# Batch 0's second group of heads goes in front of all other tasks, u's squares by halves, more casts on GpSimd, other ranks

## The chip, the cores and the metric

One core of one Trainium2 chip runs the kernel as one program. The time is the device time of an execution in microseconds, the median of several; lower is better. Engines are named as in the profile: PE (TensorE, matmuls), PEld (its weight loads), DVE (VectorE), ACT (ScalarE), POOL (GpSimd) and SP (SyncE, which issues the DMAs).

## The reference

Three stages in sequence. Attention with a forget gate over 4 batches, 8 heads, 576 positions and 64 columns; then a token and channel mixer; then a gated convolution block:

```python
scores = scale * np.matmul(q, k.transpose(0, 1, 3, 2))
decay = cum[:, :, :, None] - cum[:, :, None, :]        # cum: running sum of log f
scores = np.where(causal, -1000000000.0, scores + decay)
attn = np.exp(scores - max); attn = attn / (sum + 1e-09)
x = (attn @ v), heads side by side: (4, 576, 512)

h = np.maximum(xt @ w_tok1, 0.0) @ w_tok2              # xt: x with positions last; 576 -> 256 -> 576
u = x + h.transpose(0, 2, 1)
x = u + np.maximum(u @ w_ch1, 0.0) @ w_ch2             # 512 -> 1536 -> 512

h = np.maximum(x @ w_in, 0.0)                          # 512 -> 1024
gate = 1.0 / (1.0 + np.exp(-conv_out))                 # conv_out: 3 taps along the positions
out = (h * gate) @ w_out                               # 1024 -> 512
```

(The lines are shortened to what is computed.)

## The kernel before

All large products are made of float16 parts: every factor is split into a high part (a cast) and a low part (what the cast left), and `mm3` (L280 to L284) issues three matmuls for one: high by high (L282), high by low (L283), low by high (L284).

**Heads.** The 32 heads come in pairs (`pair`), and four heads make a group; two groups make a batch. A head's scores come from PE (L1004, L1008); DVE takes a masked maximum by row block (L1022, output t and m); ACT takes the exponential (L1028). Heads 0 to 7 (batch 0) are transposed by PE in float32. For later heads POOL casts t to its high part ph in two pieces of 1024 and 640 columns (`hi_part`, L1037), DVE makes the low part pl in the same two pieces (`lo_part`, L1043), and SP transposes both by DMA. PE multiplies by the group's values (PV; L1093 for heads 0 to 7, L1098 to L1100 later). DVE divides by the row sums (`norm`, L1107, L1108) and writes the head's part of x (`xout`, L1116, tile xf). x is then split: xh by POOL (L274) for heads below `XHP` = 8 and by ACT (L271) for the others, xl by POOL (L277), and POOL scales xf in place (`x_scale`, L1138). The group's values vp are split by POOL as well: three casts (L274) and three subtractions (L916).

**Groups.** `group(g)` holds the token mixer. Its first product T1 needs the xh and xl of four heads; T2 the two halves of T1's output. `u_copy` (ACT, L1261) takes T2 out of PSUM into us, `u_squares` (ACT, L1270, output junk) sums the squares of 1152 columns into one column of um. After a batch's second group `u_span` lets PE spread um's two columns over the partitions (the helper at L262, one matmul for each column), and `u_scale` (DVE, L251 to L257) makes a power of two of them, by which ACT (L610, uh) and DVE (L613, ul) split u.

**Channel mixer.** It runs in three parts of the 1536 columns. For one part M1 multiplies u by five column blocks of w_ch1; its output r is taken out of PSUM by ACT (high, L662) and DVE (low, L666). M2 multiplies r by the five row blocks of w_ch2. The weights of a part are staged by `weight_set`: loaded by SP, decoded by ACT (L319) and DVE (L323, L324), squared for their scale (L520), then scaled and split. For batch 0's first part the ch1 weights are scaled, cast and split by POOL (L555, L274, L277; five blocks, into the slots w10, w0, w1, w2, w3), the ch2 weights by ACT (L570) and DVE (L574; slots w4 to w8).

**What sets the order.** Each step is a task with an engine, an estimated time, a rank, and what it reads and writes. The class `Order` at the top plays the tasks through: in `run` each engine offers the open task that can start first, ties going to the lower rank, and the earliest offer of all engines is taken. The tasks are then emitted in that order, so every engine has one fixed queue, and an instruction whose input is late holds up all that stand behind it. Ranks of a head grow with its number; a group's tasks have t0 = (4g + 3) * `PER` + 6. `SETR` and `LATER` are added to t0 for the staging of the weights: `SETR` for batch 0's first part (ch1, ch2), `LATER` for the batches' further parts, and the steps 4.0 and 2.5 in the call of `weight_set` spread the five blocks.

## Time and profile before

| what | us |
|---|---|
| three runs | 717.93, 715.51, 716.53 |
| median | 716.53 |
| the profiled execution | 717.09 |
| its span, first to last instruction | 715.3 |
| PE busy | 693.4 |
| DVE busy | 501.8 |
| ACT busy | 429.7 |
| POOL busy | 266.2 |

The profiled execution is one further run; its trace gives starts and durations of all instructions in microseconds from the span's start. In a row `out<-in` are the names of the tiles, then partitions x elements and types. Where an engine sat idle before an instruction, the square brackets say how long and what released it. A busy PE counts from the start of a matmul to its modelled end; matmuls that follow each other start 0.12 us apart at 288 columns though each is shown with 0.29.

### The profile page before, as it was taken

The numbers are of one execution on the slowest core, as the hardware profiler recorded it, in microseconds if no ns is written. First come the engines' busy times: TensorE is split into PE (matmuls) and PEld (weight loads), VectorE is DVE, ScalarE is ACT, GpSimd is POOL, SyncE is SP. The second block draws the span as 40 slices with busy tenths as digits, with TensorE's granted clock in tenths as the row PEclk, the third lists the DMA queues.
The fourth block names the chain that finished last, engine by engine and source line by source line (L and its number), as shares of the span: only waits on it lengthen the run. The fifth ranks groups of instructions, "written<-read, shape, count | busy, mean of one in ns | idle before, by whom it ended". The sixth has DMA issues, their size and how long they took to land.

```text
span 715.3 us, 16400 instructions
## 1 busy us (share of the span) xinstructions
PE 693.4 (97%) x6417; PEld 559.4 (78%) x6417; DVE 501.8 (70%) x1255; ACT 429.7 (60%) x942; POOL 266.2 (37%) x344
## 2 busy tenths in 40 slices
PE   7999897799999999999999999999999999999998
PEld 6888676587778787887888778778878778778786
DVE  5778989998876788436666856635778866875570
ACT  5777886576845685555674544312177766676671
POOL 2145898657682867230000222102023222323240
PEclk9999999999999999999999999999999999999999
DMA  9435899799995987875454855345211121100101
GB/s 203 148 93 176 212 275 186 143 249 244 231 225 123 220 165 178 220 256 157 151 180 124 284 187 164 100 134 160 66 42 58 51 59 35 57 20 26 34 18 51
DMA packets 152974, 101.99 MB, mean 143 GB/s; under 512 B 89984, under 2 KB 145024, under 8 KB 152896
## 3 DMA queue, kind: packets, MB, share of 16 engines
q1 hardware_dynamic: 152896, 100.94, 54.6%
q8 instruction: 50, 0.82, 0.5%
q14 instruction: 28, 0.23, 0.1%
HBM read 57.73 MB, written 23.59 MB: 114 GB/s over the span
## 4 chain that ended last, share of the span: by engine, by line
PE 82%; DVE 7%; POOL 5%; ACT 2%; issue 2%; DMA 1%; SPq 0%; DVEq 0%; POOLq 0%; ACTq 0%
PE w L282 14%; PE w L283 14%; PE w L284 14%; PE z L283 8%; PE z L282 8%; PE z L284 8%; PE z L1004 5%; PE w L1093 3%; PE w L1245 2%; POOL vp L916 2%; PE z L1008 1%; POOL vp L274 1%; DVE pl L1043 1%; ACT t L1028 1%; PE w L1099 1%
## 5 line engine op out<-in xcount | busy, mean ns | idle before, releaser
L284 PEld LDWEIGHTS <-w 128*128 128x128 f16 x1280 | 125.3, 98 | 34.9 <-DVE w L574 3.2
L282 PEld LDWEIGHTS <-w 128*128 128x128 f16 x1280 | 124.9, 98 | 34.4 <-issue 2.7
L283 PEld LDWEIGHTS <-w 128*128 128x128 f16 x1280 | 125.0, 98 | 34.3 <-issue 3.5
L282 PE MATMUL w<-uh,w 128*128 128x288 f16 x416 | 119.0, 286 | 1.2 <-DVE r L666 1.2
L284 PE MATMUL w<-uh,w 128*128 128x288 f16 x416 | 119.0, 286 | 0.0
L283 PE MATMUL w<-ul,w 128*128 128x288 f16 x416 | 119.0, 286 | 0.0
L277 POOL TENSOR_TENSOR g<-sg,g 128x286 f16<-128x286 f32 (+1 forms) x64 | 55.1, 867 | 150.2 <-ACT g L271 148.5
L1530 DVE SCALAR_TENSOR_TENSOR cv<-hp,cw,cv 128x286 f32<-128x286 f32 (+1 forms) x128 | 75.1, 594 | 38.2 <-ACT cv L1524 36.0
L662 ACT ACTIVATE r<-w 128x288 f16<-128x288 f32 x96 | 39.2, 408 | 87.9 <-PE w L284 87.7
L1028 ACT ACTIVATE t<-t,m 128x576 f32<-128x576 f32 (+4 forms) x160 | 81.3, 552 | 17.3 <-DVE m L1022 17.2
L739 POOL TENSOR_TENSOR p<-p,u 128x288 f32<-128x288 f32 x32 | 27.3, 883 | 150.1 <-DVE wraw L323 78.1
L1022 DVE CUSTOM_DVE_ANT_0 t<-z,mask 128x576 f32<-128x576 f32 (+4 forms) x160 | 69.9, 478 | 11.1 <-PE z L1008 11.0
L666 DVE SCALAR_TENSOR_TENSOR r<-w,r 128x288 f16<-128x288 f32 x96 | 43.4, 453 | 47.4 <-ACT r L662 46.6
L283 PE MATMUL z<-g,w 128*128 128x286 f16 (+1 forms) x256 | 73.3, 286 | 0.0
L282 PE MATMUL z<-g,w 128*128 128x286 f16 (+1 forms) x256 | 73.0, 285 | 0.0
L284 PE MATMUL z<-g,w 128*128 128x286 f16 (+1 forms) x256 | 72.9, 285 | 0.0
L284 PE MATMUL w<-vh,w 128*128 128x288 f16 x224 | 64.1, 286 | 0.0
L282 PE MATMUL z<-r,w 128*128 128x288 f16 x224 | 64.1, 286 | 0.0
L283 PE MATMUL w<-vl,w 128*128 128x288 f16 x224 | 64.1, 286 | 0.0
L284 PE MATMUL z<-r,w 128*128 128x288 f16 x224 | 64.1, 286 | 0.0
L282 PE MATMUL w<-vh,w 128*128 128x288 f16 x224 | 64.1, 286 | 0.0
L283 PE MATMUL z<-r,w 128*128 128x288 f16 x224 | 64.1, 286 | 0.0
(206 smaller groups left out, 1699.8 us busy)
## 6 DMA issues: line engine op xcount, KB each, us to landing
wraw<-in_moe_w_ch_dram SPq DMA_DIRECT2D x24, 512.0 KB, 4.7
qk<-in_qk_dram SPq DMA_DIRECT2D x16, 608.0 KB, 5.1
u_d<-us SPq DMA_DIRECT2D x8, 576.0 KB, 4.5
p_d<-res SPq DMA_DIRECT2D x32, 144.0 KB, 3.6
p<-p_d SPq DMA_DIRECT2D x8, 576.0 KB, 5.4
u<-u_d SPq DMA_DIRECT2D x8, 576.0 KB, 4.9
x_d<-p SPq DMA_DIRECT2D x8, 576.0 KB, 3.4
u<-x_d SPq DMA_DIRECT2D x8, 576.0 KB, 3.9
```

What stands on the lines that cost most here:

```text
L277: nc.gpsimd.tensor_tensor(o, a, b, ALU.subtract)
L282: nc.tensor.matmul(ps, wh, xh, start=(first and i == 0), stop=False)
L283: nc.tensor.matmul(ps, wh, xl, start=False, stop=False)
L284: nc.tensor.matmul(ps, wl, xh, start=False, stop=(last and i == n - 1))
L662: nc.scalar.activation(out=t[:, 0, :], in_=box["z", m], func=AF.Relu)
L666: nc.vector.scalar_tensor_tensor(t[:, 1, :], box["z", m], 0.0, f32(t[:, 0, :]), ALU.max, ALU.subtract)
L739: nc.gpsimd.tensor_tensor(box["p"][:, d], box["p"][:, d], box["u"][:, d], ALU.add)
L1004: nc.tensor.matmul(out_[x], t[r, Q0[i]:Q0[i] + 128], t[r, k0:k0 + n], start=first, stop=False)
L1022: nc.vector.tensor_tensor_reduce(to, z_t.pop((n, i)), mk, -0.125, 3e38, ALU.add, ALU.min, m_t[n][0:rows, i:i + 1])
L1028: nc.scalar.activation(out=tt[0:rows, o:o + w], in_=tt[0:rows, o:o + w], func=AF.Exp, bias=m_t[n][0:rows, i:i + 1], scale=-1.0)
L1093: nc.tensor.matmul(o[:, 0:65], p32(n)[:, 128 * blk:128 * blk + 128], vp32_t[g % 2][:, slot, hh, :], start=(j == 0), stop=(j == nb - 1))
L1530: nc.vector.scalar_tensor_tensor(cv, hp_t[m][:, s0 + t:s1 + t], cw[:, t, m:m + 1], cv, ALU.mult, ALU.add)
```

## The change

It has five parts.

1. `Order` gets a table `WAIT` by engine, all of it 0.0, and `run` picks in two steps: the earliest possible start on the engine plus `WAIT`, and among the tasks that can start by then the one of lowest rank.
2. `AHEAD` = 60 is taken from the rank of batch 0's second group (g == GB - 1, heads 4 to 7): of the heads' PV, norm, xout, xh, xl and scaling, and of t0 in `group`.
3. `XHP` is 12 in place of 8: the xh of heads 8 to 11 is made by POOL.
4. `SETR` is (10, 30) in place of (-20, 0) with steps of 2.0 in place of 4.0 and 2.5; `LATER` is (0, 30, 50) in place of (-30, 10, 30).
5. `u_squares` runs for each half of u (576 columns) with a column of um of its own; `u_span` spreads four columns and `u_scale` sums 512.

```diff
+    WAIT = {"PE": 0.0, "DVE": 0.0, "ACT": 0.0, "POOL": 0.0, "SP": 0.0, "-": 0.0}
...
-                pick = None
+                starts = []
                 for k in ks:
                     r = ready[k]
                     if takes[k]:
                         r = max(r, slot(k))
-                    if r >= far:
-                        continue
-                    c = (max(r, at), self.tasks[k][2], k)
-                    if pick is None or c < pick:
-                        pick = c
-                if pick and (best is None or pick[0] < best[0]):
-                    best = (pick[0], pick[2], e)
+                    if r < far:
+                        starts.append((max(r, at), self.tasks[k][2], k))
+                if not starts:
+                    continue
+
+                until_ = min(starts)[0] + self.WAIT[e]
+                pick = min((c[1], c[0], c[2]) for c in starts if c[0] <= until_)
+                if best is None or pick[1] < best[0]:
+                    best = (pick[1], pick[2], e)
...
-    XHP = 8
+    AHEAD = 60.0
+    XHP = 12
-    SETR = ((-20.0, 0.0),)
-    LATER = (-30.0, 10.0, 30.0)
+    SETR = ((10.0, 30.0),)
+    LATER = (0.0, 30.0, 50.0)
...
-    um = [const.tile([128, GB], F32, name=f"um{b}") for b in range(B)]
+    um = [const.tile([128, GB * NDM], F32, name=f"um{b}") for b in range(B)]
...
+                if g == GB - 1:
+                    rank -= AHEAD
...
-            nc.scalar.activation(out=junk[:, 0:NDM * S], in_=tok[g]["u"].rearrange("p d s -> p (d s)"), func=AF.Square,
-                                 accum_out=um[g // GB][:, g % GB:g % GB + 1])
+            at = NDM * (g % GB) + d
+            nc.scalar.activation(out=junk[:, 0:S], in_=tok[g]["u"][:, d], func=AF.Square,
+                                 accum_out=um[g // GB][:, at:at + 1])
...
-            um_t[b] = spread(um[b], GB)
+            um_t[b] = spread(um[b], GB * NDM)
-            power_of_root(su[b], um_t[b], 128 * GB, 2.0)
+            power_of_root(su[b], um_t[b], 128 * GB * NDM, 2.0)
...
+            if g == GB - 1:
+                t0 -= AHEAD
...
+                T("ACT", 0.8, t0 + 4, u_squares, g, d, reads=[("us", g % 2, d, e) for e in range(2)],
+                  writes=[("junk",), ("um", b, half, d)], pools=A1)
-            T("ACT", 1.15, t0 + 4, u_squares, g, reads=uk, writes=[("junk",), ("um", b, half)], pools=A1)
...
-                                [q + 4.0 * k for k in range(n)], [q + 4.0 * n + 2.5 * k for k in range(n)], factor, ONP[y])
+                                [q + 2.0 * k for k in range(n)], [q + 2.0 * n + 2.0 * k for k in range(n)], factor, ONP[y])
```

What that does to the queues shows at three places. Lines of the kernel after are 5 higher from about L250 on, and 7 to 11 higher behind L1250; the numbers behind the tiles' names differ between the two.

**POOL, while batch 0's channel weights are split and the heads of batch 1 begin.** ph is the high part of a head (first head 10, from t2, then head 11, from t3), w0 to w3 are weights of ch1, vp the values of a group (vp1: group 3), xh, xl and xf heads 8 to 11. Before:

```order
L277 TENSOR_TENSOR w0_113<-w1_114,w0_113 128x512
L1037 TENSOR_SCALAR ph_1385<-t2_190 128x1024
L274 TENSOR_SCALAR w1_114<-w2_115 128x512
L1037 TENSOR_SCALAR ph_1385<-t2_190 128x640
L277 TENSOR_TENSOR w1_114<-w2_115,w1_114 128x512
L277 TENSOR_TENSOR xl_1490<-xf_1433,xh_1486 128x5x64
L274 TENSOR_SCALAR w2_115<-w3_116 128x512
L1138 TENSOR_SCALAR xf_1433<-xf_1433,tac_218 128x5x64
L277 TENSOR_TENSOR w2_115<-w3_116,w2_115 128x512
L1037 TENSOR_SCALAR ph_1540<-t3_191 128x1024
L274 TENSOR_SCALAR w3_116<-w4_117 128x512
L1037 TENSOR_SCALAR ph_1540<-t3_191 128x640
```

After, two pieces that follow each other:

```order
L1042 TENSOR_SCALAR ph_1447<-t2_190 128x1024
L282 TENSOR_TENSOR w0_113<-w1_114,w0_113 128x512
L279 TENSOR_SCALAR xh_1484<-xf_1471 128x5x64 x2
L282 TENSOR_TENSOR xl_1497<-xf_1471,xh_1484 128x5x64 x2
L1143 TENSOR_SCALAR xf_1471<-xf_1471,tac_218 128x5x64 x2
```

```order
L279 TENSOR_SCALAR w1_114<-w2_115 128x512
L1042 TENSOR_SCALAR ph_1447<-t2_190 128x640
L282 TENSOR_TENSOR w1_114<-w2_115,w1_114 128x512
L560 TENSOR_SCALAR w3_116<-w3_116,pw_c10_226 128x512
L279 TENSOR_SCALAR vp1_201<-vf_1331 64x4x64 x2
L279 TENSOR_SCALAR vp1_201<-vf_1331 128x16x64
L921 TENSOR_TENSOR vp1_201<-vf_1331,vp1_201 64x4x64 x2
L921 TENSOR_TENSOR vp1_201<-vf_1331,vp1_201 128x16x64
L279 TENSOR_SCALAR w2_115<-w3_116 128x512
L560 TENSOR_SCALAR w4_117<-w4_117,pw_c10_226 128x512
L282 TENSOR_TENSOR w2_115<-w3_116,w2_115 128x512
L1042 TENSOR_SCALAR ph_1656<-t3_191 128x1024
```

The xh of heads 8 and 9 stands in POOL's queue now, and the six instructions of group 3's values, which stood nine rows behind the low part written to w2, stand ahead of it and of head 11's ph.

**DVE, at the low part pl of head 11 (from t3).** r is the output of M1, xf a head's part of x, wraw and w8, w9 weights of ch2 being decoded, the lines with m the score maxima. Before:

```order
L1043 SCALAR_TENSOR_TENSOR pl_1527<-t2_190,ph_1385 128x1024
L666 SCALAR_TENSOR_TENSOR r_1522<-w_1492,r_1522 128x288
L1116 TENSOR_TENSOR xf_1433<-w_1397,rs_1513 128x5x64
L1043 SCALAR_TENSOR_TENSOR pl_1527<-t2_190,ph_1385 128x640
L1043 SCALAR_TENSOR_TENSOR pl_1557<-t3_191,ph_1540 128x1024
L666 SCALAR_TENSOR_TENSOR r_1548<-w_1516,r_1548 128x288
L666 SCALAR_TENSOR_TENSOR r_1572<-w_1544,r_1572 128x288
```

After:

```order
L1027 ISA m_1310 128x1
L328 TENSOR_SCALAR wraw_1562<-wraw_1562 128x512
L329 SCALAR_TENSOR_TENSOR w9_122<-w9_122,wraw_1562 128x512
L1027 ISA t2_190,m_1653<-z_1631,mask_131 128x576
L1027 ISA m_1653 128x1
L543 TENSOR_REDUCE stat_c20_227<-stat_c20_227 128x1
L1048 SCALAR_TENSOR_TENSOR pl_1675<-t3_191,ph_1656 128x1024
```

Head 11's pl followed head 10's at once; now decoding of weights and score maxima of batch 1's next heads stand ahead of it.

**PE, around group 2's first token matmul T1 (xh, xl by w1h, w1l).** w4 to w8 hold ch2's weights: r by them is M2; qk, dec and sel make scores. Before:

```order
L284 LDWEIGHTS w8_121
L284 MATMUL w_1891<-r_1635,w8_121 128x288
L1004 MATMUL z_1922<-qk1_149 128x64 x2
L1004 MATMUL z_1922<-qk1_149 128x448 x2
L1008 MATMUL z_1922<-dec_133,sel_134 128x512 x2
L1004 MATMUL z_1934<-qk1_149 128x192 x2
L1004 MATMUL z_1934<-qk1_149 128x320 x2
L1008 MATMUL z_1934<-dec_133,sel_134 128x512 x2
L282 LDWEIGHTS w1h_212
L282 MATMUL w_1948<-xh_1486,w1h_212 128x256
L283 LDWEIGHTS w1h_212
L283 MATMUL w_1948<-xl_1490,w1h_212 128x256
```

After:

```order
L287 LDWEIGHTS w1h_212
L287 MATMUL w_1966<-xh_1484,w1h_212 128x256
L288 LDWEIGHTS w1h_212
L288 MATMUL w_1966<-xl_1497,w1h_212 128x256
L289 LDWEIGHTS w1l_213
L289 MATMUL w_1966<-xh_1484,w1l_213 128x256
L287 LDWEIGHTS w4_117
L287 MATMUL w_1991<-r_1492,w4_117 128x288
L288 LDWEIGHTS w4_117
L288 MATMUL w_1991<-r_1492,w4_117 128x288
L289 LDWEIGHTS w4_117
L289 MATMUL w_1991<-r_1492,w4_117 128x288
```

Before, the M2 triples of the part (r by w4 to w8, the last of them here) end ahead of T1; now T1 ends ahead of the first M2 triple.

## Rows read from the trace of the kernel before

**Rows 1.** The page: span, then busy time, share and instructions of each engine.

```profile
span 715.3 us, 16400 instructions
...
PE 693.4 (97%) x6417; PEld 559.4 (78%) x6417; DVE 501.8 (70%) x1255; ACT 429.7 (60%) x942; POOL 266.2 (37%) x344
```

**Rows 2.** Table of stretches: length, busy PE PEld DVE ACT POOL (instructions), clock, DMA.

```profile
80.00:100.00 20.00, 16.83 (x136) 13.11 (x135) 17.21 (x48) 16.80 (x35) 19.17 (x25) 1.00 1.02 256
100.00:120.00 20.00, 15.49 (x188) 12.28 (x189) 19.48 (x44) 12.71 (x26) 17.08 (x17) 1.00 1.01 228
120.00:141.00 21.00, 17.19 (x206) 13.25 (x203) 20.07 (x47) 12.23 (x27) 15.08 (x14) 1.00 0.72 131
...
142.00:250.00 108.00, 106.28 (x1282) 85.37 (x1281) 85.69 (x258) 72.91 (x151) 69.81 (x71) 1.00 1.00 217
```

**Rows 3.** Timeline of PE: start, us, instruction, [idle before <-releaser].

```profile
86.99 0.27 PE L283 MATMUL w<-xl,w1h 128*128 128x256 f16 x1 [2.65 <-POOL xl L277]
...
100.16 0.49 PE L262 MATMUL w<-ident,um 128*128 128x128 f32 x2 [0.68 <-ACT junk L1270]
...
113.31 0.46 PE L262 MATMUL w<-ident,vacc 128*128 128x128 f32 x2 [2.48 <-DVE r L666]
...
117.15 0.28 PE L282 MATMUL w<-uh,w 128*128 128x288 f16 x1 [1.18 <-DVE r L666]
...
131.07 0.30 PE L284 MATMUL w<-r,w 128*128 128x288 f16 x1 [2.93 <-DVE w L574]
...
141.14 0.28 PE L282 MATMUL w<-xh,w1h 128*128 128x256 f16 x1
```

**Rows 4.** Lines of POOL: kind xcount: ns min/median/max, first and last start, shapes.

```profile
L277 POOL TENSOR_TENSOR xl<-xf,xh x32: 786/800/1772, 24.3 to 302.6; 128x320 f16<-128x320 f32 x32
L277 POOL TENSOR_TENSOR w<-w,w x5: 1153/1615/1718, 90.7 to 113.9; 128x512 f16<-128x512 f32 x5
...
L274 POOL TENSOR_SCALAR xh<-xf x8: 452/468/888, 23.7 to 83.4; 128x320 f16<-128x320 f32 x8
L274 POOL TENSOR_SCALAR w<-w x5: 611/620/1578, 89.4 to 111.7; 128x512 f16<-128x512 f32 x5
...
L1037 POOL TENSOR_SCALAR ph<-t x46: 717/1044/2200, 76.7 to 279.9; 128x1024 f16<-128x1024 f32 x23, 128x640 f16<-128x640 f32 x23
...
L1138 POOL TENSOR_SCALAR xf<-xf,tac x32: 527/542/1631, 63.9 to 303.5; 128x320 f32<-128x320 f32 x32
...
L555 POOL TENSOR_SCALAR w<-w,pw_c x5: 687/693/1249, 87.6 to 93.1; 128x512 f32<-128x512 f32 x5
```

**Rows 5.** Timeline of POOL, columns as in the timeline of PE.

```profile
93.91 2.44 POOL L274 TENSOR_SCALAR vp<-vf 64x256 f16<-64x256 f32 x3
96.32 3.59 POOL L916 TENSOR_TENSOR vp<-vf,vp 64x256 f16<-64x256 f32 x3
...
110.69 1.04 POOL L1037 TENSOR_SCALAR ph<-t 128x1024 f16<-128x1024 f32 x1
```

**Rows 6.** Line L1043 of DVE in min/median/max, then four rows of its timeline.

```profile
L1043 DVE SCALAR_TENSOR_TENSOR pl<-t,ph x46: 783/1219/2172, 77.7 to 284.1; 128x1024 f16<-128x1024 f32 x23, 128x640 f16<-128x640 f32 x23
...
77.74 1.23 DVE L1043 SCALAR_TENSOR_TENSOR pl<-t,ph 128x1024 f16<-128x1024 f32 x1 [0.15 <-POOL ph L1037]
...
103.35 0.49 DVE L1116 TENSOR_TENSOR xf<-w,rs 128x320 f32<-128x320 f32 x1
...
120.15 0.62 DVE L1022 CUSTOM_DVE_ANT_0 t<-z,mask 128x448 f32<-128x448 f32 x1
...
137.42 0.48 DVE L1116 TENSOR_TENSOR xf<-w,rs 128x320 f32<-128x320 f32 x1
```

**Rows 7.** PE: line L284 from 120 to 142; timeline at 317, a two-column spread.

```profile
L284 PE MATMUL w<-r,w x15: 286/286/296, 126.1 to 137.7; 128*128 128x288 f16 x15
...
317.33 0.61 PE L262 MATMUL w<-ident,um 128*128 128x128 f32 x4
317.78 0.29 PE L282 MATMUL w<-uh,w 128*128 128x288 f16 x1
```

More of the change, by code (lines that the diff above doesn't have):

```diff
@@ L1266, in u_back, with u_squares @@
             tok[g]["back"] = t
-        def u_squares(g):
+        def u_squares(g, d):
             junk = ap1.tile([128, NS * HG * D], U8, tag="junk", name="junk")
-            nc.scalar.activation(out=junk[:, 0:NDM * S], in_=tok[g]["u"].rearrange("p d s -> p (d s)"), func=AF.Square,
-                                 accum_out=um[g // GB][:, g % GB:g % GB + 1])
+            at = NDM * (g % GB) + d
+            nc.scalar.activation(out=junk[:, 0:S], in_=tok[g]["u"][:, d], func=AF.Square,
+                                 accum_out=um[g // GB][:, at:at + 1])
         um_t = {}
         def u_span(b):
-            um_t[b] = spread(um[b], GB)
+            um_t[b] = spread(um[b], GB * NDM)
         def u_scale(b):
-            power_of_root(su[b], um_t[b], 128 * GB, 2.0)
+            power_of_root(su[b], um_t[b], 128 * GB * NDM, 2.0)
         def u_part(g, e, lo):
@@ L1320, in group @@
             kw = turn("w")
-            T("PE", 0.45, t0 + 4, u_span, b, reads=[("um", b, x) for x in range(GB)], writes=[kw], ring=[kw])
-            T("DVE", 1.15, t0 + 4, u_scale, b, reads=[kw], writes=[("scale", id(su[b]))], ring=[kw])
+            T("PE", 0.6, t0 + 4, u_span, b, reads=[("um", b, x, y) for x in range(GB) for y in range(NDM)], writes=[kw], ring=[kw])
+            T("DVE", 1.4, t0 + 4, u_scale, b, reads=[kw], writes=[("scale", id(su[b]))], ring=[kw])
             for x in range(EARLY):
```

## The prediction

> **What bounds the kernel now.** I read the page first: PE is busy for 693.4 of 715.3 us [rows 1], so the kernel is TensorE work with 21.9 us of holes, and a change that leaves the matmuls alone can only move the holes. Next I asked the table of stretches where the holes are. Between 80 and 141 us PE idles 3.2, 4.5 and 3.8 us, 11.5 in sum; from 142 to 250 it idles 1.7 in 108 [rows 2]. (The rest of the holes is at the start, before anything that this change moves, and in the tail.) So the only stage worth arguing about is 80 to 141: the end of batch 0's attention, its channel mixer, and the heads of batch 1. In the same rows DVE is busy 17.2 of 20, 19.5 of 20 and 20.1 of 21: from 100 on VectorE is the pace-maker, and PE's waits name it (r, w, [rows 3]). POOL is nearly as full: 19.2, 17.1, 15.1. The granted clock is 1.00 throughout, so it plays no part. Third, PE's timeline [rows 3] tells which waits these are: 2.65 for POOL's xl at group 1's first token matmul, 0.68 for ACT's squares, 2.48 and 1.18 for DVE's r in M1, 2.93 for DVE's w in M2. Stage end to watch: group 2's first token matmul, T1(g2), which starts at 141.14 and after which PE is close to saturated.
>
> **The change, part by part.**
>
> *Group 1 in front.* Its rank falls by 60, so POOL does head 7's xh and xl before other heads' ph, and the 2.65 us wait should go: the xl there waited in POOL's queue, not for data. PE then reaches heads 8 and 9 about 2.65 sooner. What that is worth depends on DVE, which has to do its work all the same: it idles 2.8 + 0.5 + 0.9 = 4.2 us from 80 to 141 [rows 2], and no lead larger than that can reach T1(g2). I take 1.4, half of the 2.8 in front of 100; the ends are 0.5 (only the idle between 100 and 120) and 4.2.
>
> *Weights staged later, group 3's values earlier on POOL.* This is what the ranks do to POOL's queue (the order of POOL in the section on the change). Before, the low part of w2 stands six rows behind that of w1's slot and is done by 110.7, when head 11's ph begins [rows 5]. Now POOL takes from the xf of heads 8 and 9: two xh, two xl, two xf scalings, w high, a ph part, w low, a scaled weight, the six instructions of group 3's vp, w high, a scaled weight, w low. With medians [rows 4]: 0.94 + 1.60 + 1.08 + 0.62 + 0.72 + 1.62 + 0.69 = 7.27 (for the 640 part of ph its shortest, 0.72); vp costs 2.44 + 3.59 = 6.03 [rows 5]; then 0.62 + 0.69 + 1.62 = 2.93: 16.2 in sum. The two xf stand in DVE's queue about where head 8's xf stood, which ended at 103.85 [rows 6]. So w2's low part is there at about 120.1 and head 11's first ph part, 1.04 later, at 121.1. By the shortest rows the chain is 15.1, by the longest over 23, since POOL's instructions stretch up to twofold [rows 4].
>
> *Who waits for that.* DVE: its low part pl of head 11 now stands in its queue where before it was at about 120.2 (the maximum at 120.15 [rows 6]). With medians it waits 0.9; with the stretch that these instructions mostly have in this crowded stage (w low 1.6 against 1.15, xl up to 1.77) the chain is some 18 and the wait about 3. I take 2.2, ends 0 and 5. Queued behind pl on DVE are r of M1 (for which PE waits) and the later scores' maxima.
>
> *Other DVE work ahead of T1(g2).* Head 11's xf ends at 137.90 [rows 6]. In the new order two low parts of ch2's weights (about 0.85 each, estimated between the 0.78 and 1.22 of pl's line) go behind it and three score maxima (0.62 with the row at 120.15, somewhat more for full width) come ahead: +0.6. After xf come xh and xl, both on POOL now, 0.47 + 0.80 = 1.3. T1(g2) starts at 137.9 + 0.6 + 2.2 - 1.4 + 1.3 = 140.6, 0.5 earlier than before.
>
> *PE work moved over that point.* This decides. Before, 15 M2 triples lie ahead of T1(g2) [rows 7], each three matmuls 0.12 apart, 5.5 us; in the new order the first M2 stands behind it (order of PE). Head 12's PV (45 matmuls, some 1.4) and two more spreads (0.45) come ahead instead. So PE arrives with 5.5 - 1.4 - 0.45 = 3.65 us less work done, 0.5 us earlier: net 3.1 us more holes. Holes are lost for good on an engine that is full afterwards.
>
> *Later holes.* Of the 1.7 us between 142 and 250 I take half as covered by the M2 stock that now stands behind T1(g2): -0.9 (ends -1.7 and 0).
>
> *Squares by halves.* The spread of um grows from two to four matmuls: at 317 two take 0.45 (317.33 to 317.78 [rows 7]), so the six in batches 1 to 3 add 1.35 us of PE work (batch 0's two are counted above). What it could give is at most the 0.68 wait at um [rows 3]; ACT's second half must still follow the last copy and DVE's sum now reads 512 columns in place of 256, which eats it: 0.
>
> *Four x_hi from ACT to POOL.* 0.47 each [rows 4], two of them inside the chain above, two ahead of T1(g2), all counted. ACT is busy 12 to 13 of 20 us there [rows 2], so what it loses is worth 0.
>
> *LATER's ranks, planner costs, the rewritten pick.* With every WAIT at 0 the pick takes the earliest start and then the lowest rank, as before: 0. The later weights of each batch move behind by 20 to 30 units of rank; from 142 to 250 PE waits 1.7 us in all for anything, which is the cover, and their loads move behind on SP's queue with them, where no wait in [rows 3] names a DMA; if it were gone, each late low part would cost about its own length, 0.8.
>
> **Sum.** 3.1 - 0.9 + 1.35 = +3.55. The profiled execution took 717.09 (span 715.3 and 1.8 around it): 720.65. It lies 0.56 above the median 716.53, so the forecast for a median is 720.1.
>
> A rule to weigh: pl's 1024 columns took 1.23 at 77.74 and the longest 2.17 [rows 6], in a kernel where POOL is full from 80 to 120 [rows 2]. The Trainium skill, "SBUF — State Buffer", section "Who interferes with whom", says why: a VectorE instruction with two SBUF inputs and a GpSimd instruction that reads SBUF exclude each other, and whoever starts second waits for the whole of the other. The spread of the row agrees in direction. By that rule four more casts on GpSimd may also cost VectorE up to 4 x 0.47 = 1.9 us, and the forecast would be 722.0.
>
> **Rivals.**
>
> *Faster: the lead counts in full.* If all of DVE's 4.2 us of idle between 80 and 141 closes up and POOL's chain is done before DVE asks (chain at 15.1, ph at 120.0 or sooner), T1(g2) starts at 137.9 + 0.6 - 4.2 + 1.3 = 135.6, 5.5 earlier; holes 3.65 - 5.5 = -1.9; with -1.7 later and +1.35: -2.2, a median of 714.3. For it: a wait of 2.65 does go. Against it: DVE from 100 on has only 1.4 idle to give, and POOL gets more to do, not less, before 120.
>
> *No change.* Lead 2.8, DVE's wait 1.1: T1(g2) at 138.1, holes +0.6, sum +1.05: 717.6. This is also where it ends if the late weights simply fall into places where PE had waited for r anyway.
>
> *Slower by more: POOL becomes the bound.* The vp block ahead of w2's low part makes POOL set M1's pace: each of its instructions at nearer its longest than its median, chain 20 us or more, DVE waiting 5, lead 0.5. T1(g2) at 144.3, holes +6.8, nothing regained later: +8.2, 724.7. It decides once POOL's chain ends later than DVE reaches pl of head 11 by more than 3 us.
>
> **Numbers.** Chances: forecast (718.7 to 722) 0.35, no change 0.28, faster 0.17, slower by more 0.20. Faster or slower by over 0.3% (about what can be measured here) means below 714.4 and above 718.7: faster 0.17, same 0.28, slower 0.55. The range runs from 713.6, just past the faster rival, to 724.7, the slow one's price.
>
> **What would show it.** In the trace of the changed kernel: (1) the 2.65 wait for xl at group 1's T1 is gone, T1(g1) some 2.7 us earlier; (2) PE waits in M1 for POOL's w (a weight's low part) or for r behind DVE's wait, and DVE waits for POOL's ph of head 11 near 120; (3) T1(g2) starts between 139 and 143 with no M2 ahead of it; (4) PE's idle between 80 and T1(g2) grows from 11.5 to about 15, less than 1 us of holes from there to 250; (5) the two-column spreads become four at 0.45 more each, the clock stays at 1.00. I am wrong if T1(g2) comes before 138 (DVE had more to give), if PE is idle no longer than before up to it, or if batch 1 opens holes that this trace doesn't show.

## Result and profile after

| | us | runs |
|---|---|---|
| before, measured beside it | 716.07 (715.51 to 717.93) | 4 |
| after | 726.53 (725.05 to 728.10) | 4 |
| ratio after / before | 1.0142, 95% interval 1.0111 to 1.0173 | |
| before, measured beside the last experiments | 717.65 (715.39 to 722.27) | 29 |
| after, unaltered, measured there again | 725.39 (723.12 to 726.25) | 4 |
| ratio | 1.0085, 95% interval 1.0059 to 1.0110 | |

The medians of after are 10.5 and 7.7 us above those of before; the forecast was 3.55. The first profiled execution of after took 728.10, the longest of its eight; the second, an experiment below (e19), took 723.12. Both are read side by side here, since what they share belongs to the change and what they don't share belongs to an execution.

The page, span and PE, of after's first profile (compare [rows 1]):

```profile
span 726.3 us, 16442 instructions
...
PE 702.8 (97%) x6433; PEld 565.1 (78%) x6433; DVE 495.4 (68%) x1255; ACT 431.9 (59%) x954; POOL 261.5 (36%) x348
```

and of its second:

```profile
span 721.3 us, 16442 instructions
...
PE 695.8 (96%) x6433; PEld 560.9 (78%) x6433; DVE 496.3 (69%) x1255; ACT 431.7 (60%) x954; POOL 262.3 (36%) x348
```

PE is busy with the same instructions for 7.0 us longer in the first. It is idle for 23.5 us in the first and 25.5 in the second, against 21.9 before. The table of stretches says where the first differs; columns as in [rows 2], the clock is the last but two. First profile:

```profile
80.00:100.00 20.00, 18.65 (x151) 14.49 (x150) 15.52 (x47) 16.81 (x37) 14.73 (x21) 1.00 0.93 235
100.00:120.00 20.00, 16.27 (x183) 11.94 (x182) 18.87 (x47) 13.26 (x26) 18.66 (x22) 0.91 0.80 225
120.00:141.00 21.00, 15.31 (x173) 10.95 (x170) 18.07 (x41) 11.42 (x25) 18.91 (x18) 0.92 0.84 178
141.00:160.00 19.00, 14.92 (x143) 11.39 (x140) 15.67 (x36) 10.32 (x25) 9.20 (x9) 0.91 0.80 169
```

Second profile:

```profile
80.00:100.00 20.00, 18.68 (x221) 15.12 (x219) 15.39 (x53) 17.13 (x38) 14.73 (x22) 1.00 0.92 238
100.00:120.00 20.00, 14.04 (x106) 9.73 (x105) 19.53 (x46) 14.19 (x30) 18.51 (x19) 1.00 0.78 207
120.00:141.00 21.00, 14.24 (x198) 10.67 (x196) 18.49 (x35) 8.78 (x17) 16.95 (x17) 0.92 0.80 204
```

From 80 to 141 PE idles 10.8 us in the first and 14.0 in the second, where before it idled 11.5. Timeline of PE, first profile (columns as in [rows 3]): the first token matmuls of groups 0 and 2 and the waits between them:

```profile
54.75 0.27 PE L287 MATMUL w<-xh,w1h 128*128 128x256 f16 x1
...
116.60 0.42 PE L289 MATMUL w<-uh,w 128*128 128x288 f16 x1 [1.40 <-POOL w L282]
116.81 0.45 PE L287 MATMUL w<-uh,w 128*128 128x288 f16 x1
117.05 0.45 PE L288 MATMUL w<-ul,w 128*128 128x288 f16 x1
...
145.92 0.27 PE L287 MATMUL w<-xh,w1h 128*128 128x256 f16 x1 [3.47 <-POOL xh L279]
...
147.52 0.42 PE L287 MATMUL w<-xh,w1h 128*128 128x256 f16 x1
147.74 0.42 PE L288 MATMUL w<-xl,w1h 128*128 128x256 f16 x1
```

The same in the second profile:

```profile
51.43 0.27 PE L287 MATMUL w<-xh,w1h 128*128 128x256 f16 x1
...
82.21 0.28 PE L287 MATMUL w<-xh,w1h 128*128 128x256 f16 x1
...
111.42 0.30 PE L287 MATMUL w<-uh,w 128*128 128x288 f16 x1 [1.61 <-POOL w L279]
113.23 0.30 PE L289 MATMUL w<-uh,w 128*128 128x288 f16 x1 [1.40 <-POOL w L282]
118.33 1.49 PE L1009 MATMUL z<-qk 64*128 64x288 f32 x6 [2.23 <-issue]
...
123.50 0.30 PE L289 MATMUL w<-uh,w 128*128 128x288 f16 x1 [1.88 <-POOL w L282]
134.91 1.89 PE L1009 MATMUL z<-qk 64*128 64x192 f32 x8 [3.86 <-DVE m L1027]
142.62 0.27 PE L287 MATMUL w<-xh,w1h 128*128 128x256 f16 x1 [1.94 <-POOL xh L279]
```

The reader is to see four things. Group 1's wait of 2.65 for xl [rows 3] is gone. PE now waits in M1 for POOL's weights (1.61, 1.40, 1.88), and ahead of scores: 3.86 for a bank that DVE's maximum frees, and 2.23, for which the row names no releaser. The holes stand at the same instructions in both profiles. And in the first, matmuls of 288 columns start 0.24 apart behind the 1.40 hole (116.81, 117.05) and those of 256 columns 0.22 apart behind T1's (147.52, 147.74): half the usual rate, the lower of the clock's two levels (1.2 and 2.4 GHz); the granted clock of these stretches is 0.91 and 0.92. At 120 to 141 the second has such a 0.92 too: its trace has the lower clock from 135.1 on for 3.4 us. Below, such a time at half rate is called a slow stretch.

### The profile page after: what moved, and what is told of

The parts are those of the page before. It is cut to its first block, busy times and chain, and to the rows that moved or that the text cites. A ratio compares the mean times of both kernels' runs of the same rounds, so it can differ in the third digit from the quotient of the medians.

```text
span 726.3 us, 16442 instructions
## 1 busy us (share of the span) xinstructions
PE 702.8 (97%) x6433; PEld 565.1 (78%) x6433; DVE 495.4 (68%) x1255; ACT 431.9 (59%) x954; POOL 261.5 (36%) x348
## 4 chain that ended last, share of the span: by engine, by line
PE 86%; POOL 6%; DVE 4%; DMA 1%; issue 1%; ACT 1%; SPq 0%; DVEq 0%; ACTq 0%; POOLq 0%
PE w L287 15%; PE w L288 15%; PE w L289 15%; PE z L288 8%; PE z L287 8%; PE z L289 8%; PE z L1009 6%; PE w L1098 3%; PE w L1252 2%; PE z L1013 1%; PE w L267 1%; PE w L1066 1%; PE w L1104 1%; PE w L1103 1%; PE w L1105 1%
## 5 line engine op out<-in xcount | busy, mean ns | idle before, releaser
L289 PE MATMUL w<-uh,w 128*128 128x288 f16 x416 | 120.4, 289 | 3.2 <-POOL w L282 3.2
L287 PE MATMUL w<-uh,w 128*128 128x288 f16 x416 | 120.4, 289 | 1.6 <-POOL w L279 1.6
L1033 ACT ACTIVATE t<-t,m 128x192 f32<-128x192 f32 (+4 forms) x160 | 81.5, 552 | 20.9 <-DVE m L1027 17.9
L1027 DVE CUSTOM_DVE_ANT_0 t<-z,mask 128x320 f32<-128x320 f32 (+4 forms) x160 | 70.2, 479 | 23.6 <-PE z L1013 23.5
L744 POOL TENSOR_TENSOR p<-p,u 128x288 f32<-128x288 f32 x32 | 25.7, 836 | 150.4 <-DVE w L579 88.2
L1009 PE MATMUL z<-qk 64*128 64x288 f32 (+4 forms) x384 | 60.6, 430 | 6.5 <-DVE m L1027 3.5
L287 PE MATMUL z<-r,w 128*128 128x288 f16 x224 | 64.1, 286 | 0.0
L288 PE MATMUL z<-r,w 128*128 128x288 f16 x224 | 64.1, 286 | 0.0
## 6 DMA issues: line engine op xcount, KB each, us to landing
u_d<-us SPq DMA_DIRECT2D x8, 576.0 KB, 4.1
p<-p_d SPq DMA_DIRECT2D x8, 576.0 KB, 4.8
u<-u_d SPq DMA_DIRECT2D x8, 576.0 KB, 5.9
x_d<-p SPq DMA_DIRECT2D x8, 576.0 KB, 3.2
u<-x_d SPq DMA_DIRECT2D x8, 576.0 KB, 3.9
```

Of the source, the lines that this page charges most:

```text
L287: nc.tensor.matmul(ps, wh, xh, start=(first and i == 0), stop=False)
L288: nc.tensor.matmul(ps, wh, xl, start=False, stop=False)
L289: nc.tensor.matmul(ps, wl, xh, start=False, stop=(last and i == n - 1))
L744: nc.gpsimd.tensor_tensor(box["p"][:, d], box["p"][:, d], box["u"][:, d], ALU.add)
L1009: nc.tensor.matmul(out_[x], t[r, Q0[i]:Q0[i] + 128], t[r, k0:k0 + n], start=first, stop=False)
L1027: nc.vector.tensor_tensor_reduce(to, z_t.pop((n, i)), mk, -0.125, 3e38, ALU.add, ALU.min, m_t[n][0:rows, i:i + 1])
```

## Experiments

Ratios are against runs of before on the same chip. The last column leaves out the start: it is the profiled span less the start of group 0's first token matmul, T1(g0), and is 663.9 and 663.7 in two profiles of before. In the kernels with group 1 in front (after, e9, e1, e3, e4) 363 matmuls stand ahead of T1(g0) in place of 351: twelve more of PV. They take 1.3 us (T1(g0) starts at 51.43 in after's second profile and at 50.07 to 50.09 in e5, e10, e11 and e14, none of which has a slow stretch before it), so 1.3 has to be added to the last column of those five when they are compared with the others.

| kernel | median us | ratio (95%) | clock, span of the profile | T1(g0) to the end |
|---|---|---|---|---|
| after, first | 726.53 | 1.0142 (1.0111, 1.0173) | 0.993, 726.3 | 671.6 |
| after, second | 725.39 | 1.0085 (1.0059, 1.0110) | 0.998, 721.3 | 669.9 |
| e20 before again | 718.40 | 0.9994 (0.9972, 1.0017) | 0.998, 715.0 | 663.7 |
| e9 group 1 ahead only | 729.99 | 1.0159 (1.0129, 1.0189) | 0.983, 728.1 | 674.6 |
| e2 ranks only | 729.19 | 1.0159 (1.0127, 1.0191) | 0.986, 727.7 | 675.3 |
| e11 halves only | 723.41 | 1.0070 (1.0044, 1.0096) | 0.998, 720.7 | 670.6 |
| e10 casts only | 717.74 | 0.9990 (0.9974, 1.0007) | 0.995, 715.1 | 665.0 |
| e1 after, ranks of before | 724.85 | 1.0102 (1.0073, 1.0131) | 0.988, 724.3 | 670.8 |
| e5 after, group 1 not ahead | 725.52 | 1.0114 (1.0078, 1.0151) | 0.992, 722.6 | 672.5 |
| e12 one estimate +0.05 | 722.45 | 1.0045 (1.0026, 1.0065) | 0.992, 721.4 | 668.3 |
| e13 one estimate +0.04 | 721.46 | 1.0045 (1.0023, 1.0067) | 0.985, 720.7 | 668.6 |
| e3 short vp | 726.48 | 1.0130 (1.0099, 1.0160) | 0.984, 726.8 | 672.0 |
| e4 after, three holes filled | 724.51 | 1.0091 (1.0055, 1.0127) | 0.988, 724.3 | 670.9 |
| e14 short hole at 460 | 719.47 | 1.0025 (1.0004, 1.0046) | 0.993, 717.0 | 666.9 |
| e15 long hole at 460 | 725.34 | 1.0099 (1.0064, 1.0134) | 0.990, 723.9 | 670.9 |
| e16 before, three holes filled | 716.41 | 0.9974 (0.9956, 0.9992) | 0.995, 715.7 | 663.7 |
| e18 casts, one hole filled | 718.32 | 1.0001 (0.9987, 1.0015) | 0.990, 717.2 | 665.1 |

**Second profiles.** Both kernels, unaltered (e19 is after, e20 before).

> The changed kernel unaltered, for a second profile of it. Theory A (the holes of the stretch from 80 to 150 us belong to the change, the clock's fall behind them to the execution): the holes stand at the same instructions within 0.5 us each, 13 to 16 us between 80 and 150; of the stretches at the lower clock the places differ from the first profile's, and the late start of the first profile (2 us) is gone. Rival B (the clock's falls belong to the change): the same three stretches behind the same three holes. Time 724 to 728 either way.

> The kernel before unaltered, for a second profile of it. Theory A: the same holes (2.65, 2.48, 2.93 at the same instructions), behind one or more of them matmuls at twice the spacing in this execution, and a span longer by some 1.7 us for each. Rival B: no stretch at the lower clock behind any of them, span 713 to 716.

Theory A of e19 holds: the holes are the change's (the same instructions, most within 0.1 us; in the second profile the two score holes are 0.9 and 1.3 longer and T1(g2)'s is 1.5 shorter), the place of the lower clock is the execution's. Theory A of e20 failed: no slow stretch stands behind any of before's three holes, in either profile. Each has its only one at the start, from 10.1 and from 9.9. What the two profiles of after differ by can be followed: T1(g0) starts at 54.75 and at 51.43 (3.3), T1(g2) at 145.92 and 142.62 (still 3.3), the ends at 726.3 and 721.3 (5.0). So the two slow stretches between 116 and 130 of the first profile, some 1.7 us each, cost nothing at T1(g2): the score holes behind them are shorter by about as much. Nor does the second profile's own, at 135, where T1(g2)'s hole is shorter by 1.5: from T1(g1) to T1(g2) it is 60.39 in the first and 60.41 in the second, and DVE's xf of head 11 stands the same 3.3 apart (144.41 and 141.11). The stretch behind T1(g2), where PE has few holes left, goes with 1.7 more (580.4 to the end against 578.7). And 3.3 arose in the first 55 us, in the same queue of the same kernel. The scores at the start, first profile of after:

```profile
7.70 2.29 PE L1009 MATMUL z<-qk 64*128 64x288 f32 x8 [1.65 <-DMA qk<-in_qk_dram]
11.44 2.29 PE L1009 MATMUL z<-qk 64*128 64x64 f32 x8 [0.98 <-DVE m L1027]
```

second profile of after:

```profile
7.45 1.24 PE L1009 MATMUL z<-qk 64*128 64x288 f32 x8 [1.63 <-DMA qk<-in_qk_dram]
10.02 1.25 PE L1009 MATMUL z<-qk 64*128 64x64 f32 x8 [0.97 <-DVE m L1027]
```

and before:

```profile
7.63 1.24 PE L1004 MATMUL z<-qk 64*128 64x288 f32 x8 [1.58 <-DMA qk<-in_qk_dram]
10.10 2.29 PE L1004 MATMUL z<-qk 64*128 64x64 f32 x8 [0.97 <-DVE m L1022]
```

Eight of these matmuls take 1.24 or 2.29 with nothing changed but the execution. (For 7 to 17 in after's first profile the table of stretches says 1.00 all the same: this trace's record of the clock begins at 17.4, so its mean of 0.993 leaves the slow start out.) T1(g0) lay between 50.07 and 54.82 over all profiles here.

**One part alone.** Group 1 ahead, and the ranks:

```diff
+    AHEAD = 60.0      # e9; used as in the change
-    SETR = ((-20.0, 0.0),)       # e2, with its steps
+    SETR = ((10.0, 30.0),)
-    LATER = (-30.0, 10.0, 30.0)
+    LATER = (0.0, 30.0, 50.0)
```

> The kernel before with group 1 in front alone. Theory A (each part has its own price, the holes are made by late weights): the 2.65 wait at group 1's T1 goes and the time is 713 to 717. Theory B (the order before is a narrow optimum, and whatever reshuffles the queues costs some 6 to 11 us because PE's granted clock then falls behind the holes of the stage 80 to 150): 722 to 729, with stretches of low clock between 80 and 160.

> The kernel before with the new weight ranks alone. Theory (late weights do it): 721 to 726, PE waits for POOL's w in M1, granted clock about 0.9 between 100 and 150. Rival (the parts only hurt together, or another part does it): 715 to 718.

Each costs at least as much alone (ratio 1.0159 for both) as all parts together (1.0142 and 1.0085), and both medians lie above what their theories gave (729 and 726 at most). In e9 PE waits for score banks, which DVE's maxima free, and for ACT's uh:

```profile
98.85 1.46 PE L1005 MATMUL z<-qk 64*128 64x64 f32 x7 [3.72 <-DVE m L1023]
105.82 0.28 PE L283 MATMUL w<-uh,w 128*128 128x288 f16 x1 [2.14 <-ACT uh L611]
```

In e2 it waits for a weight's low part, which the ranks bring to POOL later:

```profile
125.92 0.42 PE L284 MATMUL w<-uh,w 128*128 128x288 f16 x1 [5.83 <-POOL w L277]
```

The halves (the change's fifth part) and the casts:

```diff
-                T("ACT", 1.15, t0 + 4, u_squares, g, ...              # e11, with um, u_span and u_scale
+                    T("ACT", 0.8, t0 + 4, u_squares, g, d, ...
-    XHP = 8                                                # e10
+    XHP = 12
```

> The kernel before with u's squares by halves alone. Theory A: eight more spread matmuls, 1.8 us on PE, less up to 0.7 of the wait at um: 717 to 719. Theory B (any reshuffled order costs): 722 to 729.

> The kernel before with the four more casts on POOL alone. Theory A: four casts of 0.47 on POOL, at most 2 us: 716 to 719. Theory B (any reshuffled order costs): 722 to 729.

The casts are free: no change within 0.3%. The halves, priced at 1.35 us of spreads, cost 5 us (the ratio's 0.7%), though the mean clock of their profile is 0.998. Their estimates (0.8 twice for 1.15, 0.6 for 0.45, 1.4 for 1.15) move the queues, and new holes open (2.20 for DVE's ul, 1.79 for POOL's xl).

**All parts but one.** The ranks back (e1), group 1 not ahead (e5):

```diff
-    SETR = ((10.0, 30.0),)       # e1, with its steps, of the kernel after
+    SETR = ((-20.0, 0.0),)
-    LATER = (0.0, 30.0, 50.0)
+    LATER = (-30.0, 10.0, 30.0)
-    AHEAD = 60.0                 # e5, of the kernel after
+    AHEAD = 0.0
```

> The changed kernel with the three sets of weight ranks (SETR, its two steps, LATER) as before; group 1 in front, 12 casts on POOL and the halved squares stay. Theory: the late weights on POOL's queue make the holes in M1, and the granted clock falls to its lower level behind them. With the ranks back PE waits for no weight in M1 between 105 and 130, the clock stays at 1.00 in the stage 100 to 150, and the time comes back to 716 to 719. Rival (group 1 in front, or the casts, make the holes): the time stays at 723 or more and the clock in that stage at 0.9.

> The changed kernel without group 1 in front (weight ranks, casts and halved squares stay). If parts had prices that add, it would be worth what the changed kernel is less the price of that part alone (1.6%): about 715. Theory (prices don't add; late weights make holes in M1, behind which the clock falls): 722 to 730.

Neither intervals nor medians come back to before. The prices of the parts don't add (1.6 + 1.6 + 0.7 + 0 in per cent, 0.9 to 1.4 together), so no single part carries the loss. And group 1 in front brings nothing that can be measured: without it (e5) the median is 725.52, with it 726.53 and 725.39.

**A price for any new order.** One estimate of the planner raised by 0.05 or 0.04, which computes nothing else and only moves queues:

```diff
-            T("DVE", 1.1, rank, v_pow, ...       # e12
+            T("DVE", 1.15, rank, v_pow, ...
-                T("DVE", 0.46, rank + 6, xout, ...   # e13
+                T("DVE", 0.5, rank + 6, xout, ...
```

> A control: the kernel before with the planner's estimate for one DVE step (the power of two of a group's values) at 1.15 in place of 1.10, which changes no instruction but moves instructions in the queues from the middle of the program on. Theory A (parts have their own price): 715 to 718. Theory B (the order before is a narrow optimum): 722 to 729, with PE's clock down in the stage 80 to 160.

> A second control: the kernel before with the planner's estimate of one DVE step (xout) at 0.50 in place of 0.46; no instruction changes, the queues are reshuffled. Theory (the order before is a narrow optimum): 720 to 729. Rival (a reshuffle as such costs nothing): 715 to 718.

Both cost 0.45%, some 3 us, for no reason of their own. The casts alone, whose four instructions change queue, cost nothing (e10). So a neighbour of before's order can be that much worse; three don't say how often.

**The vp block on POOL.** Group 3's values are split for 1 of 64 columns (the rest stays zero, so the work of 63 is left out), which shortens POOL's chain ahead of w2's low part:

```diff
+            if t is vp_t[1]:
+                nc.gpsimd.memset(t, 0.0)
...
+            if g == 3:
+                hi, low, t = hi[:, :, :, 0:1], low[:, :, :, 0:1], t[:, :, :, 0:1]
```

> The changed kernel, with group 3's values split for one column in 64 only (the rest of that tile is zero, so heads 12 to 15 are left out in effect); same order, about 5 us less on POOL ahead of the low part of w2. Theory (POOL's chain sets M1's pace): the wait of 1.8 for that low part at 126.7 goes, the second stretch of low clock with it, T1 of group 2 starts 3 to 5 us earlier, total 721 to 724. Rival (DVE sets the pace whatever POOL does): T1 of group 2 moves by less than 1.5 us, total 725 to 727.

The hole at w2's low part (1.81 and 1.88 in after's profiles) goes, and so does DVE's wait for head 11's ph. T1(g2) doesn't come earlier: from T1(g0) it is 91.6 us, against 91.2 in both profiles of after. But e3's execution has a slow stretch from 92.8 on, over the start of group 1's second product, and DVE waits 1.2 us longer for the scores behind that product (4.27; 3.05 in after). Counted from the xf of heads 8 and 9, where POOL's chain starts, T1(g2) is 35.7 us away (110.74 to 146.44) in place of 37.1 (105.51 to 142.62):

```profile
109.86 0.88 DVE L1125 TENSOR_TENSOR xf<-w,rs 128x320 f32<-128x320 f32 x2
```

So the vp block on POOL is worth some 1.4 us of T1(g2), by this one profile.

**The lower clock.** After, with 24, 14 and 26 matmuls that compute nothing new ahead of M1's first two waits and of T1(g2) (e4):

```diff
+            if c == 0 and part == 0 and k == 0 and m in (ms[2], ms[3]):
+                for _ in range(24 if m == ms[2] else 14):
+                    nc.tensor.matmul(box["z", m], fh[:, 0, :], uh[:, 0, :], start=True, stop=True)
+            if g == 2 and a == 0:
+                for _ in range(26):
+                    nc.tensor.matmul(st["ps1", a], w1h[:, 1, c], w1l[:, 1, :], start=True, stop=True)
```

> The changed kernel with matmuls put into three holes: 24 ahead of M1's block on w1, 14 ahead of that on w2, 26 ahead of group 2's T1, each writing into the bank that the waiting block then starts afresh; some 7.5 us of PE work that should fit into the waits (3.0, 1.8, 3.5 us). Theory (the low clock behind the holes costs time of its own): granted clock back to 1.00 in most of 110 to 152, time 3 to 5 us less than the changed kernel, 721 to 724. Rival (the slow stretches are hidden by the next wait, so that only the holes count): no gain or a loss, 726 to 729.

The median fell by 2 us, between what theory and rival gave, but not for this: two of its four runs had a clock of 0.998 and took 723.07 and 723.06, and after's run at 0.998 took 723.12. At the same clock the fillers are worth nothing that can be measured. Nor is the test a clean one: in e4's profile a slow stretch lies over the 14 fillers (from 122.0), another stands behind a score hole (from 135.7), and the 26 hold up T1(g2) to 146.31 though its xh is there at 144.5. What the lower clock costs after isn't settled by it. Then an idle of PE's own making late in the kernel, where nothing else differs: the last r of a chunk written 8 times (e14) or 13 times (e15) by DVE.

```diff
+            for _ in range(8 if c == 5 and part == 1 and m == ms[-1] else 1):
```

> The price of one hole by itself: the kernel before, its queues unchanged, with one low part r on DVE of the sixth chunk's second part issued 8 times in place of once (7 x 0.45 = 3.2 us more on DVE, in the stretch where PE is saturated). PE's M2 of that block waits for it. Theory (the clock falls behind a hole): a hole of some 1.5 us in PE's timeline, followed or not by a stretch at the lower clock (0.24 in place of 0.12 between matmuls); the time grows by the hole, and by 1.7 more if the clock falls: +1.5 to +3.2. Rival (a hole costs its own length only, or less): +1.5 at most.

> As the short hole, with the low part issued 13 times (5.4 us more on DVE): a hole of some 3.7 us. Theory: behind it matmuls stand 0.24 apart for some 3.4 us, which costs 1.7 more than the hole: +5 to +6. Rival (the hole alone): +3.7, matmuls 0.12 apart right behind it.

PE at that place in e14, then in e15:

```profile
462.74 0.28 PE L283 MATMUL z<-r,w 128*128 128x288 f16 x1 [1.74 <-DVE r L667]
```

```profile
468.32 0.40 PE L283 MATMUL z<-r,w 128*128 128x288 f16 x1 [4.20 <-DVE r L667]
468.51 0.45 PE L284 MATMUL z<-r,w 128*128 128x288 f16 x1
468.75 0.44 PE L282 MATMUL z<-r,w 128*128 128x288 f16 x1
```

Behind 4.20 the rate is halved, behind 1.74 not; but the length alone doesn't decide, for in e15 the kernel's own hole of 2.48, the one of [rows 3], is followed by slow matmuls too, where before has 0.12 between them:

```profile
115.69 0.46 PE L262 MATMUL w<-ident,vacc 128*128 128x128 f32 x2 [2.48 <-DVE r L667]
...
116.40 0.45 PE L284 MATMUL w<-uh,w 128*128 128x288 f16 x1
116.64 0.45 PE L282 MATMUL w<-uh,w 128*128 128x288 f16 x1
```

There it costs: e15 has three slow stretches ahead of T1(g2) (from 88.7, 116.1 and 133.1), and T1(g0) to T1(g2) takes 91.2 in place of 89.7 in both profiles of before. From T1(g2) to the end e14 takes 1.9 us more than before (576.0 against 574.1) and e15 5.6 more (579.7): the hole of 1.74 alone, and the hole of 4.20 with 1.4 on top, near the 1.7 that the theory gives for the slow stretch behind it. Over the whole kernel the ratios are 1.8 and 7.1 us. Last, before and the casts with fillers in before's own holes:

```diff
+            if g == 1 and a == 0:                # e16, e18
+                for _ in range(22):
+                    nc.tensor.matmul(st["ps1", a], w1h[:, 1, c], w1l[:, 1, :], start=True, stop=True)
+            if c == 0 and part == 0 and k == 0 and m == ms[1]:     # e16
+                for _ in range(12):
+                    nc.tensor.matmul(box["z", m], fh[:, 0, :], uh[:, 0, :], start=True, stop=True)
+            if c == 0 and part == 0 and d == 0 and m == ms[-1]:    # e16, zero weights
+                for _ in range(22):
+                    nc.tensor.matmul(box["o", d], vp_t[0][64:128, 0, 0, 0:128], box["r", ms[0]][64:128, 0, :],
+                                     start=False, stop=False)
```

> The kernel before with matmuls that compute nothing new, where its trace shows TensorE idle: 22 of 256 columns (some 0.11 us apart, 2.4 us) ahead of group 1's first stage (idle 2.65 at 86.99), 12 of 288 columns ahead of the second group of first-product matmuls (ahead of the idle 2.48 at 113.31), 22 of 288 columns with zero weights in the second product where it waits for the fifth low part (idle 2.93 at 131.07). Nothing of the result changes. Theory A (a hole costs its own length and, in some executions, a stretch of some 3.4 us at the lower clock behind it, some 1.7 us): no more holes of over 1.5 us there and no lower clock behind them, so the slower executions of before vanish: median 0 to 3 us lower than before's of the same call, and a narrower spread. Rival B (the clock falls for another cause, or the fillers push the chains behind them): the same median or up to 3 us more.

> The kernel before with the four more high parts of x on GpSimd (the change's own part, measured alone at 0.999), and the same 22 matmuls of 256 columns ahead of group 1's first stage. Theory A: 0 to 2 us under before (ratio 0.997 to 1.000). Rival B: 1.000 to 1.004.

The idle is filled in e16 (0.41 is left where 2.93 was, behind the 22 fillers):

```profile
131.50 0.30 PE L284 MATMUL w<-r,w 128*128 128x288 f16 x1 [0.41 <-DVE w L574]
```

e16 is the fastest kernel measured here, 0.26% below before, with an interval that just excludes 1. At a clock of 1.000 it takes 714.99 to 715.68 and before 715.39 to 715.73, the same; its slowest run is 719.12, before's 722.27. So what it gains, if anything, is fewer slow stretches, as A has it; with 12 runs this is not shown. e18 gains nothing.

## Why the prediction was off

**The direction held, the mechanism in part.** Its signs: (1) the 2.65 wait is gone. T1(g1) starts at 82.21, 1.7 us earlier than in e20 (83.89), but only 0.3 earlier than in e14, whose start, like that of after's second profile, has no slow stretch:

```profile
50.09 0.27 PE L282 MATMUL w<-xh,w1h 128*128 128x256 f16 x1
...
82.53 0.27 PE L282 MATMUL w<-xh,w1h 128*128 128x256 f16 x1
```

(The wait stood behind T1(g1)'s first matmul, so this start could not show it.) (2) PE waits for POOL's w, and DVE for head 11's ph, 1.67 of the 2.2 taken. (3) T1(g2) starts at 142.62 in the second profile, inside 139 to 143, with no M2 ahead of it (in the first, after its late start, at 145.92). The work moved over it is as forecast: ahead of it PE has 45 matmuls of M2 fewer, 45 of PV more and four more of um. (4) From 80 to T1(g2) PE idles 15.7 us (1.3, 6.0, 6.8 and 1.6 up to 142.62), as forecast "about 15", against 11.5; from there to 250 only 0.6. (5) The spreads of um:

```profile
L262 PE MATMUL w<-ident,um 128*128 128x128 f32 x16 | 3.0, 299 | 0.7 <-ACT junk L1270 0.7
```

before, and after

```profile
L267 PE MATMUL w<-ident,um 128*128 128x128 f32 x32 | 4.5, 284 | 0.0
```

"The clock stays at 1.00" was wrong.

**The sum, at an equal start.** The mean clock is 0.998 in after's second profile and in e20, and the two are 6.3 us apart (721.3 against 715.0). But that is not an equal loss: e20's slow stretch delays T1(g0) by 1.2 (51.32; 50.09 in e14, whose queue is the same up to there), and after's, at 135, costs nothing. Beside before's runs at a clock of 1.000 (715.39 to 715.73) after's 723.12 is 7.4 to 7.7 slower, where the sum said 3.55. Without its slow stretch before's T1(g2) would be at 50.09 + 89.7 = 139.8, and the forecast, 0.5 earlier, at 139.3; it came at 142.62, 3.3 later. From T1(g2) to the end it takes 578.7 in place of 574.1, +4.6, where 3.65 - 0.9 + 1.35 = 4.1 were put. That difference is a slip in the sum: batch 0's two more spreads (0.45) were taken off the work that moves behind T1(g2), but they are new work, not moved work. With 5.5 - 1.4 = 4.1 in place of 3.65 the part behind T1(g2) is 4.55 and the whole sum 4.0. (A smaller slip, on which nothing rests: w2's low part stood four rows behind that of w1's slot, not six.)

**The term that failed: the lead of 1.4.** It was taken out of DVE's idle of 2.8 before 100, on the view that group 1 in front brings heads 8 and 9 sooner and that DVE then closes up. The opposite came: from T1(g1) to T1(g2) DVE is busy for 53.7 us, as long as in both profiles of before (53.8), but it is idle for 6.75 in place of 3.26, and the whole takes 60.4 in place of 57.1. The forecast had DVE's idle grow by 0.8 (the wait of 2.2 less the lead of 1.4); it grew by 3.5. Two waits are the largest part of it, second profile of after:

```profile
96.20 0.76 DVE L1027 CUSTOM_DVE_ANT_0 t<-z,mask 128x576 f32<-128x576 f32 x1 [3.05 <-PE z L1013]
...
98.98 0.42 DVE L328 TENSOR_SCALAR wraw<-wraw 128x512 int32<-128x512 int32 x1
...
104.64 0.87 DVE L1121 TENSOR_TENSOR xf<-w,rs 128x320 f32<-128x320 f32 x2
...
124.49 1.62 DVE L1048 SCALAR_TENSOR_TENSOR pl<-t,ph 128x1024 f16<-128x1024 f32 x1 [1.67 <-POOL ph L1042]
...
141.11 0.48 DVE L1121 TENSOR_TENSOR xf<-w,rs 128x320 f32<-128x320 f32 x1
```

The 1.67 was in the sum, as 2.2. The 3.05 was not. DVE stands at a score maximum, whose scores PE issues only behind all of group 1's second product, and a weight's decoding (98.98) stands behind it in DVE's queue. Before, these scores stood behind that product too, but DVE was decoding weights meanwhile and came to the maximum without a wait:

```profile
98.05 2.41 DVE L324 SCALAR_TENSOR_TENSOR w<-w,wraw 128x512 int32<-128x512 int32 x1 [0.79 <-ACT w L319]
100.38 0.74 DVE L1022 CUSTOM_DVE_ANT_0 t<-z,mask 128x576 f32<-128x576 f32 x1
```

The experiments tell which part did that. The wait is there with the ranks alone (e2) and with everything but group 1 in front (e5):

```profile
99.18 0.76 DVE L1022 CUSTOM_DVE_ANT_0 t<-z,mask 128x576 f32<-128x576 f32 x1 [2.51 <-PE z L1008]
```

```profile
97.41 0.76 DVE L1027 CUSTOM_DVE_ANT_0 t<-z,mask 128x576 f32<-128x576 f32 x1 [2.50 <-PE z L1013]
```

In e3 and e4, which have the new ranks too, it is 4.27 and 3.06. In the profiles with the ranks of before, among them e9 (group 1 in front alone) and e1 (all parts but the ranks), DVE reaches this maximum with no wait of over 0.3. So the later staging of the weights took the decodings away that had filled DVE's time there. The prediction followed the ranks into POOL's queue, and into DVE's only from 120 on; what they take out of DVE's queue ahead of 100 it put at nothing. This doesn't make the ranks the whole loss: with them back (e1) the kernel is at 724.85 still, and DVE has other waits there (1.98 for ACT's t1h, 1.54 for POOL's ph). In e9, group 1 in front alone, these are 2.62 and 1.10 for t1h.

On POOL the chain was sized well: it runs from xf of heads 8 and 9, done at 105.5 where 103.9 was taken; second profile of after:

```profile
105.28 1.38 POOL L279 TENSOR_SCALAR xh<-xf 128x320 f16<-128x320 f32 x2 [1.18 <-DVE xf L1121]
...
122.29 1.15 POOL L282 TENSOR_TENSOR w<-w,w 128x512 f16<-128x512 f32 x1
...
141.68 0.89 POOL L279 TENSOR_SCALAR xh<-xf 128x320 f16<-128x320 f32 x1 [2.02 <-DVE xf L1121]
```

From xh to the end of w's low part it takes 18.2 us, the "some 18" of the prediction; it only starts 1.4 later than taken. A lead that DVE can't use is what the no-gain end, 0.5, stood for; below zero, where it came out, no bound was set.

**What the sum did not hold: the clock.** "It plays no part" rested on 1.00 in [rows 2], which begin at 80, in one execution; the same trace has a slow stretch from 10.1 on. After ran at 0.986 to 0.998 in its eight executions, before at 0.986 to 1.000. Beside the last experiments both medians lie some 2 us above the fastest run (725.39 over 723.12, 717.65 over 715.39), so the difference of 7.7 there is that of the undisturbed runs. The 10.5 of the first comparison holds some 3 us more; its four runs of after have clocks of 0.988 and 0.993. That the change makes slow stretches likelier, by more and longer holes, is possible; with eight executions of after it isn't shown.

**The rivals.** "POOL becomes the bound" gave 724.7, near the median, which is luck: it was to decide once DVE waits over 3 us for POOL's ph, and DVE waited 1.67. "No change" and "faster" fell. The rule weighed (the Trainium skill, "SBUF — State Buffer", section "Who interferes with whom") would have put up to 1.9 us on the four casts; e10 measured 0.9990 with 1.0007 as the upper end, 0.5 us, so no such price shows here.

## What to carry to other kernels

A lead given to one chain is worth only what the pace-making engine can use. Where several parts change one order, follow each of them through the whole queue of that engine: work that one part takes out of a place may have been what covered a wait there. And set the bound below zero. Read a second profile of the same kernel before a difference is put down to the change; here one execution carried 5.0 us that were not the change's. An equal mean clock doesn't make two executions comparable: look where the slow stretches lie, and what stands ahead of the mark from which time is counted. Where a planner sets the order, measure a neighbour that changes nothing: if that costs 0.45%, a part's price below that may be luck of the order, not the part.

## What was not expected of the hardware

The granted clock of the same queue differs between executions. The kernel before was measured from 715.39 at 1.000 to 722.27 at 0.988; at the start eight score matmuls took 1.24 or 2.29 us. Behind idle of 1.40 to 5.83 us PE ran for some 3.4 us at half rate (0.24 in place of 0.12 between matmuls of 288 columns) in some executions, and not behind the same idle in others (2.48: e15 yes, both profiles of before no); behind 4.20 yes, behind 1.74 no. The Trainium skill, "TensorE: Matmul & The Clock Gate", Part 1, says that the monitor of PE's activity runs freely and isn't set back at a kernel's start; that would let the same hole fall differently in each execution, but no run here shows the monitor itself, and what decides stays open. What a slow stretch costs depends on what stands behind it. Behind T1(g2), where PE has few holes left, after's went with 1.7 us; three ahead of it (two in the first profile, one in the second) cost nothing; but in e3 one from 92.8 on, ahead of scores that DVE waits for, goes with 1.2 more of that wait, and the three in e15 cost 1.5 together.
